# Gated rows of w_down kept in DRAM, and the scale of gelu times up moved into the evacuation of the up sums

## The chip, the cores and the metric

The kernel runs on one core of one Trainium2 chip. The metric is the device time of one execution in microseconds (us); before the change it is 1646.46 us, the median of 3 runs (1646.23 to 1646.75). A core has five engines that run on their own and wait for each other by semaphores: PE (matrix products, with PEld for its weight loads), DVE (vector), ACT (activations and copies with a scale), POOL (elementwise) and SP, which here issues every DMA, in the order of its queue.

## The reference, cut to what matters

```
mod = (silu(c) @ w_mod), cut into sa, ca, ga, sb, cb, gb       # rows of 512
h = layernorm(x) * (1 + ca) + sa
x = x + ga * attention(h)      # 2048 queries, 32 heads of 128, the last 512 keys of the cache
h = layernorm(x) * (1 + cb) + sb
g, u = h @ w_gate, h @ w_up    # 512 -> 1376
x = x + gb * ((gelu(g) * u) @ w_down)                          # 1376 -> 512
```

All inputs are float32. The gate gb multiplies the result's columns, so it can be multiplied into the columns of w_down beforehand.

## The kernel before, in words

**Precision.** Each float32 operand of a product is split in two float16 halves, high and low, and a product is three matmuls (high by high, high by low, low by high). ACT makes a high half by a copy, DVE or POOL makes the low half by subtraction. The operands are scaled into float16's range by powers and maxima found at run time; the scales of the feed-forward part lie in the columns of the tile `ffs`: column 2 scales w_down, column 3 goes into gelu, column 4 into the product of gelu and up, column 5 into the evacuation of the last product.

**Stages.** Attention fills about the first 1270 us: 128 iterations, each one head and 512 queries. In each, scores go to PSUM (`psS`), ACT takes the exponentials, POOL makes the low halves (`s_low`, line 921), SP transposes them by DMA into `pT` (tag with three buffers), and `pv` (line 935) multiplies them by v. The feed-forward part follows. It works on 22 units (p, f): p is one of two halves of the 2048 rows (1024 rows, as two blocks of 512), f one of 11 blocks of 128 columns of the 1376 (the last has 96). A unit's gate and up products run by Strassen-Winograd's scheme on two PSUM banks, X and Y, in four stages (`stage`, line 1686): after stages 0, 1 and 2 ACT copies the sum in X to SBUF (tile `h32`), and DVE adds Y to it into the tile `r`, whose two halves hold gelu's input or output and up. Stage 0 gives the gate of block 0, stage 2 and stage 3 give the two ups, and in stage 3 gelu reads X itself. `finish` (line 1662) multiplies gelu by up and by `ffs` column 4, and the product is split into the hidden block `hid`, or, for three pairs of units, kept in `hf` and combined further. `down` takes hid with w_down into `acc`, which DVE adds to in place (`down_add`, line 1722); a finished `acc` goes out by DMA.

**The gate in w_down.** w_down's maximum must be known before its scale is. So during attention the 11 blocks of w_down are loaded into a ring of two buffers (`raw2`; `fm_load`, line 1241), multiplied by the row gb on POOL (`fm_gate`, 1252) and reduced to their maxima on DVE (`fm_max`, 1246); the gated blocks are then dropped. In the feed-forward part `wd_load` (1469) loads each block again, `wd_gate` (1473) gates it again, `wd_high` and `wd_low` split it; `wt_make` (1625) does the same for the six blocks of the three pairs. For these gates the row gb is loaded a second time (`gate_again`, 1212), since its buffer has had another use in between.

**What sets the order.** No instruction is issued where the code calls it. `Weaver` (lines 90 to 447) records every call with its operands (`note`, 174), plays the program through a model of the engines with costs per instruction (`cost`, 150; `play`, 250), and issues it in the order of the best of several plans, some of them shaken by random numbers from a fixed seed (`issue`, 412). The plan is made in pieces: what starts before 60 us of the model is fixed first, then up to 130 us, and so on to the end. So every change to the list of calls gives a new plan from the start on. `tt` (line 982) leaves a two-tile operation to POOL or DVE, as the planner finds; a `scalar_tensor_tensor` called on `nc.vector` is DVE's. One rule of the model is used below. Between two instructions of PE, or two of SP, a dependence costs no time of its own unless the later one reads a DRAM tile:

```
def in_line(self, m, n):                                  # line 138
    return self.ops[m][0] == self.ops[n][0] and self.ops[m][0] in ("PE", "SP") and n not in self.landing
```

All instructions go out from one line (444), so rows of the profile are told apart by the tiles that they write and read, not by lines. In them `h` is the tile `h32`, `T`, `B`, `A`, `S` are the operands of the Winograd products, `st` the softmax statistics.

## Time and profile before

| what | value |
|---|---|
| median of 3 runs | 1646.46 us (1646.23 to 1646.75) |
| the profiled execution's own time | 1646.04 us |
| its span, first to last instruction | 1644.3 us |
| instructions | 24592 |
| granted clock of PE | 1.000 |
| DMA queue of SP: bytes, share of 16 engines | 230.99 MB, 70.4% |

A row of the profile by stretches gives, for a window of the span, the busy us and number of instructions of PE, PEld, DVE, ACT and POOL, PE's granted clock, the busy share of the DMA engines and GB/s. A row of a group gives the engine, the operation, out<-in with shapes, the count, then busy us and the mean ns of one, then the idle time before them and what ended it. A row of the timeline gives start and duration in us, with the idle time before it in brackets. A row of DMA issues ends with the median us from issue to landing.

### The profile page before, as it was taken

Reading aid. Unit: us, or ns where it says so; the run is one execution under the profiler, and the core shown is the slowest. Engines: PE = TensorE matmul, PEld = TensorE weight load, DVE = VectorE, ACT = ScalarE, POOL = GpSimd, SP = SyncE. Lnnn points to the kernel's source line nnn. Section 1 sums busy time; section 2 is a strip of 40 time slices with the busy share of each in tenths; the row PEclk is TensorE's granted clock in tenths of the full one; section 3 lists DMA queues with packets and bytes.
Section 4 is the critical chain, followed back from the end, with each engine's and each line's share of the span. In section 5 each row is a group of like instructions: output and inputs, shape, how many; then the busy total and the mean of one; then the engine's idle time right before and its main releaser. Section 6 shows DMA issues by size and latency. Waiting matters only on the chain.

```text
span 1644.3 us, 24592 instructions
## 1 busy us (share of the span) xinstructions
PE 1633.7 (99%) x7754; PEld 764.7 (47%) x7754; DVE 1441.0 (88%) x2644; ACT 1241.1 (75%) x2466; POOL 1119.3 (68%) x911
## 2 busy tenths in 40 slices
PE   8999999999999999999999999999999999999999
PEld 5544444444444444444444444444444444444564
DVE  8999988888888889889989898888889987897786
ACT  6977877777787887877778778778777977676553
POOL 4788766557666676775678888887655866636672
PEclk9999999999999999999999999999999999999999
DMA  8867887877787989899998988787865742321121
GB/s 243 152 130 135 150 162 130 151 137 152 141 161 143 193 148 184 169 196 179 209 175 180 181 172 175 155 166 162 159 114 92 146 98 71 75 63 46 39 74 52
DMA packets 697538, 232.55 MB, mean 141 GB/s; under 512 B 605248, under 2 KB 673920, under 8 KB 697408
## 3 DMA queue, kind: packets, MB, share of 16 engines
q1 hardware_dynamic: 697408, 230.99, 70.4%
q8 instruction: 61, 1.00, 0.3%
q14 instruction: 69, 0.57, 0.1%
HBM read 80.81 MB, written 5.38 MB: 52 GB/s over the span
## 4 chain that ended last, share of the span: by engine, by line
PE 95%; DVE 3%; DMA 1%; ACT 1%; SPq 0%; issue 0%; POOL 0%; DVEq 0%; ACTq 0%
PE psS L444 31%; PE psW L444 24%; PE psO L444 21%; PE psQ L444 18%; DVE st L444 1%; DMA acc<-in_A_x_dram 1%; DVE acc L444 1%; DMA raw<-in_A_wo_dram 0%; DMA wm<-in_w_mod_dram 0%; DVE bnst L444 0%; SPq L444 0%; ACT h L444 0%; DVE hf L444 0%; DVE B L444 0%; DVE raw L444 0%
## 5 line engine op out<-in xcount | busy, mean ns | idle before, releaser
L444 POOL TENSOR_TENSOR pp<-p,pp 128x1024 f16<-128x1024 f32 x256 | 545.2, 2130 | 309.1 <-ACT pp L444 194.5
L444 ACT ACTIVATE p<-psS,st,es 128x512 f32<-128x512 f32 x512 | 393.2, 774 | 181.1 <-DVE st L444 175.7
L444 PE MATMUL psW<-wo,oT 128*128 128x512 f16 x1536 | 417.6, 379 | 0.1
L444 DVE SCALAR_TENSOR_TENSOR acc<-psW,st,acc 128x512 f32<-128x512 f32 x496 | 366.8, 742 | 39.5 <-PE psW L444 36.9
L444 PE MATMUL psS<-kT,q 128*128 128x512 f16 x1536 | 376.9, 379 | 1.5 <-ACT q L444 1.0
L444 PE MATMUL psO<-pT,v 128*128 128x512 f16 x1536 | 377.7, 379 | 0.0
L444 DVE TENSOR_REDUCE st<-psS 128x2 f32<-128x1024 f32 x256 | 312.3, 1220 | 47.3 <-PE psS L444 47.0
L444 ACT ACTIVATE pp<-p 128x1024 f16<-128x1024 f32 x256 | 271.1, 1059 | 3.9
L444 PEld LDWEIGHTS <-q 128*128 128x128 f16 x1536 | 149.9, 98 | 181.2 <-ACT q L444 1.5
L444 PEld LDWEIGHTS <-oT 128*128 128x128 f16 x1536 | 150.2, 98 | 180.3 <-issue 0.4
L444 PEld LDWEIGHTS <-v 128*128 128x128 f16 x1536 | 150.2, 98 | 180.2 <-DMA pT<-pp 0.2
L444 PEld LDWEIGHTS <-aw 128*128 128x128 f16 (+1 forms) x840 | 84.2, 100 | 94.3 <-issue 1.8
L444 ACT ACTIVATE oT<-psO 128x512 f16<-128x512 f32 x128 | 76.1, 594 | 64.2 <-PE psO L444 63.8
L444 PE MATMUL psS<-T,aw 128*128 128x512 f16 (+1 forms) x480 | 120.4, 379 | 0.6 <-DVE r L444 0.4
L444 PE MATMUL psQ<-B,A 128*128 128x512 f16 x480 | 120.1, 379 | 0.0
L444 PE MATMUL psQ<-T,S 128*128 128x512 f16 x468 | 114.6, 379 | 0.0
L444 DVE SCALAR_TENSOR_TENSOR oT<-psO,oT 128x512 f16<-128x512 f32 x128 | 88.0, 687 | 24.4 <-ACT oT L444 24.1
L444 PEld LDWEIGHTS <-A 128*128 128x128 f16 x696 | 68.0, 98 | 81.3 <-issue 1.0
L444 ACT ACTIVATION_READ_ACCUMULATOR p<-psS,st,es 128x1 f32 x512 | 101.5, 198 | 0.0
L444 PEld LDWEIGHTS <-S 128*128 128x128 f16 x624 | 61.0, 98 | 73.7
L444 PE MATMUL psS<-B,aw 128*128 128x512 f16 (+1 forms) x360 | 90.9, 379 | 0.6 <-ACT r L444 0.6
L444 DVE TENSOR_SCALAR st<-st,es 128x1 f32<-128x1 f32 x512 | 84.8, 205 | 3.2
(275 smaller groups left out, 2326.8 us busy)
## 6 DMA issues: line engine op xcount, KB each, us to landing
raw<-in_A_k_cache_dram SPq DMA_DIRECT2D x32, 256.0 KB, 3.6
raw<-in_A_wq_dram SPq DMA_DIRECT2D x32, 256.0 KB, 3.4
raw<-in_A_v_cache_dram SPq DMA_DIRECT2D x32, 256.0 KB, 3.3
raw<-in_A_wo_dram SPq DMA_DIRECT2D x32, 256.0 KB, 3.2
pT<-pp SPq DMA_TRANSPOSE x512, 3.3
sa<-most SPq DMA_DIRECT2D x28, 256.0 KB, 3.8
raw<-in_B_w_gate_dram SPq DMA_DIRECT2D x26, 256.0 KB, 3.1
raw<-in_B_w_up_dram SPq DMA_DIRECT2D x26, 256.0 KB, 3.2
```

The source lines that it names most:

```text
L444: made[n] = real(*a, **k)
```

## The change

During attention each gated block of w_down is, after its gate, also stored by a DMA of SP into a DRAM tile of its own (`fm_keep`; 11 tiles `wg0` to `wg10`). The feed-forward part loads the blocks from there, and the 17 gates, the function `wd_gate` and the second load of gb are gone. In `finish` the product of gelu and up is a plain two-tile product, which the planner may give to POOL or DVE. Its former scale (`ffs` column 4) is applied earlier to up: ACT's copies of X after stages 1 and 2 carry it as their scale, and DVE's two sums that give up multiply Y by it.

```diff
-    MS, FF = {}, {}
+    MS = {}
...
-    def gate_again():
-        FF["gb"] = base.tile([P, D], F32, name="gb", tag="gb", bufs=1)
-        mod_row(5, FF["gb"])
...
+    WG = {}
+
+    def fm_keep(n):
+        f = n - 24
+        t = WG[f] = dram.tile([P, D], F32, name=f"wg{f}", tag=f"wg{f}", bufs=1)
+        m = min(P, DFF - f * P)
+        nc.sync.dma_start(t[:m], FM[n][:m])
+
     for n in range(len(pieces_)):
         at(s + 2 + 11 * n // 4, fm_load, n)
         if n >= 24:
             at(s + 5 + 11 * n // 4, fm_gate, n)
+            at(s + 6 + 11 * n // 4, fm_keep, n)
         at(s + 8 + 11 * n // 4, fm_max, n)
...
     def wd_load(f):
         t = FRAW["d", f] = raw_tile()
-        nc.sync.dma_start(t[:rows(f)], w_down[f * P:f * P + rows(f), :])
-
-    def wd_gate(f, eng=nc.gpsimd):
-        m = rows(f)
-        t = FRAW["d", f]
-        tt(t[:m], t[:m], FF["gb"][:m], OP.mult)
+        nc.sync.dma_start(t[:rows(f)], WG[f][:rows(f)])
...
             t = raw_tile()
-            nc.sync.dma_start(t, w_down[(f + k) * P:(f + k + 1) * P, :])
-            tt(t, t, FF["gb"], OP.mult)
+            nc.sync.dma_start(t, WG[f + k])
             raw.append(t)
...
-            nc.vector.scalar_tensor_tensor(HF[u][:, r, :], t[:, 1, :], ffs[:, 4:5], t[:, 0, :], op0=OP.mult, op1=OP.mult)
+            tt(HF[u][:, r, :], t[:, 1, :], t[:, 0, :], OP.mult)
...
-        nc.vector.scalar_tensor_tensor(t[:m, 1, :], t[:m, 1, :], ffs[:m, 4:5], t[:m, 0, :], op0=OP.mult, op1=OP.mult)
+        tt(t[:m, 1, :], t[:m, 1, :], t[:m, 0, :], OP.mult)
...
         if n < 3:
             v = UV[u, n] = right.tile([P, N], F32, name="h32", tag="h32", bufs=3)
-            nc.scalar.activation(v[:m], X, AF.Copy)
+            nc.scalar.activation(v[:m], X, AF.Copy, scale=ffs[:m, 4:5] if n else 1.0)
         if n in (0, 2):
-            t = r_tile(u, n // 2)[:m, n // 2, :]
-            nc.vector.tensor_tensor(t, Y, UV.pop((u, n))[:m], op=OP.add)
+            t, v = r_tile(u, n // 2)[:m, n // 2, :], UV.pop((u, n))[:m]
             if n == 0:
+                nc.vector.tensor_tensor(t, Y, v, op=OP.add)
                 gelu(u, 0, t)
+            else:
+                nc.vector.scalar_tensor_tensor(t, Y, ffs[:m, 4:5], v, op0=OP.mult, op1=OP.add)
         if n == 3:
-            nc.vector.tensor_tensor(RT[u, 0][:m, 1, :], Y, UV.pop((u, 1))[:m], op=OP.add)
+            nc.vector.scalar_tensor_tensor(RT[u, 0][:m, 1, :], Y, ffs[:m, 4:5], UV.pop((u, 1))[:m], op0=OP.mult, op1=OP.add)
             gelu(u, 1, X)
             finish(u, 1)
             finish(u, 0)
...
-    at(e + 9, gate_again)
...
             wd_load(w)
-            wd_gate(w)
             wd_high(w)
             wd_low(w)
```

Since the planner sets the order, the diff does not show it. Two places follow. The first is SP's queue late in the attention, where the middle blocks of w_down are loaded for their maxima; `most` and `sa` belong to the maxima of the heads' weights, and a name's number tells one tile from the next. In brackets stand the engines or DMA lanes that a row waits for. Before:

```order
L444 DMA most_2115<-mx0_79 128x4 [waits DMAHW0_49,DVE_49]
L444 DMA raw2_1918<-in_B_w_down_dram 128x512 [waits DMAHW1_49,DVE_49]
L444 DMA raw2_1953<-in_B_w_down_dram 128x512 [waits DMAHW2_49,DVE_49]
L444 DMA_TRANSPOSE pT_2081<-pp_2080 128x8x128 [waits DMAHW3_49,PE_49,Pool_49]
L444 DMA_TRANSPOSE pT_2081<-pp_2080 128x8x128 [waits DMAHW4_49]
L444 DMA sa_2134<-most_2115 128x512 [waits DMAHW5_49,DMAHW0_49]
```

After:

```order
L444 DMA raw2_1902<-in_B_w_down_dram 128x512 [waits DMAHW6_49,DMAHW3_49,DVE_49]
L444 DMA wg3_1914<-raw2_1871 128x512 [waits DMAHW7_49]
L444 DMA raw2_1922<-in_B_w_down_dram 128x512 [waits DMAHW7_49,DMAHW0_49,DVE_49]
L444 DMA_TRANSPOSE pT_2068<-pp_2067 128x8x128 [waits DMAHW1_49,PE_49,Pool_49]
L444 DMA_TRANSPOSE pT_2068<-pp_2067 128x8x128 [waits DMAHW2_49]
```

The load of raw2_1922 takes the buffer that wg3 is stored from, and waits for the lane of that store (DMAHW7), with the transposes behind it; before, a load in this ring waited for DVE's maximum only.

The second place is the end of DVE's queue, in the last unit (1, 10), whose tiles have 96 rows: `r_3458` and `r_3462` before, `r_3468` and `r_3472` after, are its gelu and up of the two blocks. Before:

```order
L444 TENSOR_TENSOR r_3458<-psS_3456,h32_3459 96x512 [waits PE_49]
L444 SCALAR_TENSOR_TENSOR r_3458<-r_3458,ffs_82 96x512 [waits DVE_49]
L444 SCALAR_TENSOR_TENSOR acc_72<-psW_3467,ffs_82,acc_72 128x512 [waits PE_49]
L444 SCALAR_TENSOR_TENSOR r_3462<-r_3462,ffs_82 96x512 [waits Activation_49]
L444 TENSOR_TENSOR hid_3464<-r_3462,hid_3464 96x512 [waits Activation_49]
L444 TENSOR_TENSOR hid_3465<-r_3458,hid_3465 96x512 [waits Activation_49]
```

After:

```order
L444 SCALAR_TENSOR_TENSOR r_3468<-psS_3466,ffs_82,h32_3469 96x512 [waits PE_49]
L444 SCALAR_TENSOR_TENSOR acc_72<-psW_3476,ffs_82,acc_72 128x512 [waits PE_49]
L444 SCALAR_TENSOR_TENSOR acc_72<-psW_3477,ffs_82,acc_72 128x512 [waits PE_49]
L444 TENSOR_TENSOR r_3472<-r_3472 96x512 [waits Activation_49]
L444 TENSOR_TENSOR hid_3474<-r_3472,hid_3474 96x512 [waits Activation_49]
L444 TENSOR_TENSOR hid_3475<-r_3468,hid_3475 96x512 [waits Activation_49]
```

The last sum now carries the scale, the product of r_3468 has left DVE (it is POOL's last instruction), and a second sum into acc stands in its place.

## Prediction

> **What bounds the kernel now.** First the page's busy times, then the same engines by stretches of the span (busy us, number of instructions, granted clock, DMA share, GB/s).

> ```profile
> span 1644.3 us, 24592 instructions
> PE 1633.7 (99%) x7754; PEld 764.7 (47%) x7754; DVE 1441.0 (88%) x2644; ACT 1241.1 (75%) x2466; POOL 1119.3 (68%) x911
> ```

> ```profile
> 0.00:41.00 41.00, 36.40 (x205) 23.77 (x206) 32.81 (x91) 25.93 (x45) 20.51 (x40) 1.00 0.85 244
> ...
> 400.00:1260.00 860.00, 860.00 (x3987) 389.80 (x3985) 762.54 (x1444) 673.58 (x1358) 617.68 (x438) 1.00 0.85 166
> 1260.00:1340.00 80.00, 79.21 (x382) 37.57 (x381) 73.56 (x137) 67.59 (x132) 54.30 (x45) 1.00 0.64 127
> 1340.00:1450.00 110.00, 110.00 (x511) 49.80 (x510) 92.57 (x141) 80.84 (x154) 69.52 (x91) 1.00 0.29 74
> 1450.00:1500.00 50.00, 48.64 (x223) 22.26 (x222) 43.79 (x66) 34.64 (x66) 23.18 (x26) 1.00 0.19 52
> 1500.00:1630.00 130.00, 130.00 (x729) 72.40 (x727) 102.37 (x152) 68.51 (x130) 82.94 (x94) 1.00 0.14 42
> 1630.00:1645.00 15.00, 10.43 (x49) 4.52 (x47) 9.47 (x14) 1.83 (x3) 0.00 (x0) 0.93 0.38 140
> 850.00:965.00 115.00, 115.00 (x535) 52.14 (x533) 102.96 (x192) 90.32 (x185) 94.38 (x70) 1.00 0.89 178
> ```

> PE is busy for 1633.7 of 1644.3 us, so only 10.6 us of it are idle. Of those, 4.6 us (41.00 - 36.40) lie in the start and 4.6 us (15.00 - 10.43) in the tail. Every stretch that the change relieves has PE at or near 100%. The idle places between are these (the number in brackets is the idle time of PE before the row, and what ended it):

> ```profile
> 1277.89 1.46 PE L444 MATMUL psQ<-T,A 128*128 128x512 f16 x6 [0.28 <-DVE h L444]
> 1323.51 0.39 PE L444 MATMUL psS<-T,B 128*128 128x512 f16 x1 [0.44 <-ACT B L444]
> 1465.15 2.75 PE L444 MATMUL psS<-B,aw 128*128 128x512 f16 x12 [0.61 <-ACT r L444]
> 1471.15 0.38 PE L444 MATMUL psS<-T,aw 128*128 128x512 f16 x1 [0.38 <-DVE r L444]
> 1471.79 0.38 PE L444 MATMUL psS<-T,aw 128*128 128x512 f16 x1 [0.26 <-POOL T L444]
> ```

> They come to 0.28 + 0.44 + 0.61 + 0.38 + 0.26 = 1.97 us. That is all that faster helpers can give back between the start and the tail.

> Does a busy PE hide waits inside the matmuls? The pace says no: 860.00 / 3987 = 215.7 ns a matmul in the attention and 110.00 / 511 = 215.3 ns in the feed-forward part, while DVE's share goes from 0.89 to 0.84 and the DMA share from 0.85 to 0.29. A pace that does not move with the helpers is PE's own. [...]

> **The change, part by part.** The prices, from the groups of 1270 to 1645 us (busy us, mean ns):

> ```profile
> L444 DVE TENSOR_TENSOR raw<-raw,gb 128x512 f32<-128x512 f32 x9 | 6.8, 760 | 0.0
> L444 DVE SCALAR_TENSOR_TENSOR r<-r,ffs 128x512 f32<-128x512 f32 x28 | 22.0, 793 | 1.9 <-ACT r L444 1.8
> L444 DVE TENSOR_TENSOR hf<-hf 128x512 f32<-128x512 f32 x8 | 5.5, 681 | 0.5 <-POOL hf L444 0.5
> L444 DVE TENSOR_TENSOR r<-psS,h 128x512 f32<-128x512 f32 x60 | 41.2, 687 | 25.2 <-ACT h L444 15.7 <-PE psS L444 8.8
> L444 DVE SCALAR_TENSOR_TENSOR acc<-psO,ffs,acc 128x512 f32<-128x512 f32 x32 | 23.8, 742 | 2.6 <-PE psO L444 2.6
> L444 POOL TENSOR_TENSOR raw<-raw,gb 128x512 f32<-128x512 f32 x7 | 8.9, 1272 | 3.5 <-DVE hf L444 2.0 <-DVE wd L444 1.5
> L444 ACT ACTIVATE h<-psS 128x512 f32<-128x512 f32 x60 | 35.6, 596 | 42.5 <-PE psS L444 42.1
> L444 ACT ACTIVATE r<-psS,ffs 128x512 f32<-128x512 f32 x20 | 13.6, 679 | 3.6 <-DVE r L444 3.3
> ```

> 1. *The 17 gates go.* The order of before has 10 on DVE and 7 on POOL: 10 x 0.760 = 7.6 us of DVE and 7 x 1.272 = 8.9 us of POOL.
> 2. *The product loses its scale.* All 44 stood on DVE: 44 x 0.79 = 34.8 us go. The order of after puts 32 on DVE and 12 on POOL. A plain product of two SBUF tiles takes between 681 ns (hf) and 760 ns (the gate) on DVE; I take 0.72: 23.0 us. POOL gets 12 x 1.272 = 15.3 us.
> 3. *The scale enters the evacuation.* 44 activations go from 596 ns to the 679 of the form with a scale from a column: 44 x 0.083 = +3.7 us of ACT. 44 sums go from 687 ns to what a scaled sum out of PSUM costs, 742: +2.4 us of DVE.

> So DVE is relieved by 7.6 + 34.8 - 23.0 - 2.4 = 17.0 us out of the 312.3 that it is busy from 1260 to 1630, ACT gets 3.7 more, and POOL 15.3 - 8.9 = 6.4 more. None of this is time by itself: PE hides all but the five waits above. Of the five I let half go in time, since the relief is on DVE, and three of them name ACT or POOL, which get more work: **-1.0 us**, bounds -1.97 (all) and +1.0 (the same waits half as long again).

> 4. *Eleven stores and what stands behind them.* Each is a DMA more on SP's queue in about 850 to 965 us. Five of the eleven (wg1, wg3, wg4, wg7, wg8) have, as the very next row, the load that reuses the buffer they read from, and that load waits for the store to land. The planner's model counts two DMAs of SP as in line (line 139), without such a wait. Behind the held queue stand the transposes that pv needs. How long does a store take to land? Nearest rows (median us from issue to landing): stores of whole rows late in the kernel, two kinds of loads in this stretch, and a scattered store a little earlier:

> ```profile
> out_dram<-acc SPq DMA_DIRECT2D x16, 256.0 KB, 2.5
> raw<-in_B_w_down_dram SPq DMA_DIRECT2D x10, 256.0 KB, 3.6
> raw<-in_A_k_cache_dram SPq DMA_DIRECT2D x3, 256.0 KB, 4.2
> msum<-ga SPq DMA_DIRECT2D x1, 256.0 KB, 5.6
> ```

> So 2.5 to 5.6 us; I take 3.6, the load of the same size in the same stretch. What can SP spare, and how late may transposes be? SP's waits in 850 to 965 us (total, times, longest; 13 rows, the first and the last shown, sum 47.0 us), then one load and four transposes on SP, the pv that uses these, and how long a transpose takes to land:

> ```profile
> SPq L444 <- POOL raw L444: 12.9, 5, 3.6
> ...
> SPq L444 <- DVE top L444: 0.4, 1, 0.4
> ```

> ```profile
> 851.54 0.52 SPq L444 DMA_DIRECT2D raw<-in_B_w_down_dram  x1
> 854.10 7.04 SPq L444 DMA_TRANSPOSE pT<-pp  x4
> ```

> ```profile
> 866.92 1.46 PE L444 MATMUL psO<-pT,v 128*128 128x512 f16 x6
> 877.28 1.46 PE L444 MATMUL psO<-pT,v 128*128 128x512 f16 x6
> ```

> ```profile
> pT<-pp SPq DMA_TRANSPOSE x47, 3.3
> ```

> SP idles 47.0 of 115 us, 4.2 us in each round of 10.4 us (877.28 - 866.92). A store and its wait take 0.5 us of issue and 3.1 of waiting, 3.6 us, of that. The last of four transposes is issued a quarter of 7.04 us before 861.14, so at 859.4, lands 3.3 us later at 862.7, and is used at 866.92: 4.2 us of slack. A hold of 3.6 us fits into either. I put **+0.5 us** for one that meets a late gate on POOL, bounds 0 and +8.5 (the rival below). The extra 11 x 0.25 MB raise 178 GB/s by 2.75 MB / 115 us = 24 GB/s to 202, under what PE has borne without a wait:

> ```profile
> 780.00:820.00 40.00, 40.00 (x187) 18.15 (x186) 38.85 (x76) 31.03 (x65) 25.42 (x19) 1.00 1.05 210
> ```

> [...]

> 5. *The second load of gb* and the loads of w_down: one load of 256 KB less, and 17 loads that read other DRAM at the same size. They are issued ahead of use by whole units: 0.

> 6. *The tail.* The last unit's hidden block is waited for there:

> ```profile
> 1630.75 0.69 DVE L444 TENSOR_TENSOR r<-psS,h 96x512 f32<-96x512 f32 x1 [2.27 <-PE psS L444]
> ...
> 1634.26 0.50 PEld L444 LDWEIGHTS <-hid 96*128 96x128 f16 x3 [0.15 <-ACT hid L444]
> ...
> 1634.98 4.96 PEld L444 LDWEIGHTS <-hid 96*128 96x128 f16 x24 [0.23 <-DVE hid L444]
> ```

> Between the last matmul into psS and the first that reads the last hid stood 18 other matmuls, and now stand 21: 3 x 0.216 = 0.65 us more cover. Against it stand 0.06 us for the longer sum; the second sum into acc that DVE now has ahead of the last product takes the place of the other product, now on POOL. So the wait of 0.15 + 0.23 goes: **-0.3 us**, bounds -0.4 and +0.5 (product late by the difference 1.272 - 0.76).

> 7. *The start* has the same 58 filling matmuls and almost the same PE order up to the first scores, since planning begins again from other random draws: 0, bounds -0.6 and +0.6.

> Sum: -1.0 + 0.5 - 0.3 = -0.8 us. The profiled execution took 1646.04 us (span 1644.3 and 1.74 around it), 0.42 below the median of 1646.46; so 1645.2 for such an execution and **1645.7 us** for the median.

> **The rivals.**

> *A. Nothing arrives.* The saved DVE time is off the path, the new order has its own few waits in other places: 1646.5. For it: the helpers are already hidden for 98% of the way. Against: two of the waits at 1465 to 1472 name r, which DVE and ACT make.

> *B. The stores hold SP.* If they land in 5.6 us as the scattered store did, a hold is 0.5 + 5.2 = 5.7 us, 1.5 over the slack of 4.2; a held gate ahead of it adds to that. Five of them cost 5 x 1.5 = 7.5 us at PE, and with one more us at the start of it 8.5; if SP's idle time takes up part, 4. Middle 6: 1652.5. It decides from a landing of about 4.2 us on. For it: DMA share 0.89 there, and the loads of k there took 4.2 us. Against: the plain stores' 2.5.

> *C. The evacuation of psS becomes what PE waits for.* If each unit's psS came free later by both increments, 44 x 0.083 + 44 x 0.055 = 6.1 us: 1652.6. Against: PE waits for r at two places in 22 units now, and the product behind it is shorter.

> *D. Waits hidden in the matmuls' pace.* If PE's busy time did hold waits, part of the 17.0 us would show; with DVE one of three helpers, I set a third: -5.7, and 1640.8. Against: the pace of 215.7 and 215.3 ns.

> **How the numbers follow.** Forecast 0.60; A 0.18; B 0.14, of which 0.09 beyond 3.3 us; C 0.05; D 0.03. 0.2% is 3.3 us, about what a measurement of this kernel can tell from no change. Faster by more: D alone, 0.03, since start, waits and tail together hold no 3.3 us that the change can reach (1.97 + 0.4 + 0.6 = 3.0). Slower by more: 0.09 + 0.05 = 0.14. Same: 0.83. The range goes from 1646.5 - 1.97 - 0.4 = 1644.1 up to 1649.8, which takes in A and the lesser part of B; outside lie D and what is 3.3 us or more slower, 0.17.

> **What would show it.** Right: PE idle in 1260 to 1630 us below 1.97 us; no wait at pv between 850 and 970 us; the stores wgN landing in about 3.6 us; DVE busy about 17 us less; no wait of PE's loads for hid in the tail. Wrong: rows psO<-pT,v or their weight loads released by a DMA with 0.5 us or more, stores that take over 4.2 us, or PE waiting for ACT h or r in many units. A different pace than 215.5 ns would break the whole working.

## The result, and the profile after

The changed kernel takes 1652.15 us, the median of 6 runs (1650.85 to 1656.6), against 1646.7 us for the kernel before beside it (6 runs, 1646.23 to 1647.15): a ratio of 1.0036, with an interval of 1.0026 to 1.0047. It is 5.45 us slower, where 1645.7 was forecast in a range up to 1649.8. The profiled execution took 1652.53 us; its page begins:

```profile
span 1650.7 us, 24575 instructions
PE 1635.2 (99%) x7754; PEld 765.2 (46%) x7754; DVE 1436.8 (87%) x2642; ACT 1231.8 (75%) x2444; POOL 1122.7 (68%) x918
```

The span grew by 6.4 us. By stretches (columns as before) it is seen where:

```profile
0.00:41.00 41.00, 36.29 (x206) 23.91 (x207) 32.69 (x90) 27.14 (x47) 19.64 (x39) 1.00 0.85 244
...
850.00:965.00 115.00, 110.05 (x502) 49.13 (x500) 97.85 (x186) 87.57 (x178) 82.09 (x60) 0.99 0.91 190
965.00:1260.00 295.00, 295.00 (x1369) 133.72 (x1367) 259.97 (x494) 226.72 (x458) 228.46 (x160) 1.00 0.81 153
```

PE stands still for 4.95 us (115.00 - 110.05) in the one stretch with the stores, where before it stood still for none, and runs 502 matmuls there in place of 535. The 33 that are missing are worth 33 x 0.2157 = 7.1 us (0.2157 us is the pace of 400 to 1260 us before): more than the idle time. PE's idle places of over 0.3 us behind the start, all of them:

```profile
44.29 0.59 PE L444 MATMUL psS<-kT,q 128*128 128x512 f16 x2 [0.53 <-ACT p L444]
930.09 1.46 PE L444 MATMUL psO<-pT,v 128*128 128x512 f16 x6 [1.35 <-DMA pT<-pp]
942.90 2.61 PE L444 MATMUL psO<-pT,v 128*128 128x512 f16 x6 [3.59 <-DMA pT<-pp]
1331.94 0.59 PE L444 MATMUL psO<-pT,v 128*128 128x512 f16 x2 [0.73 <-DMA pT<-pp]
1479.20 1.02 PE L444 MATMUL psS<-T,aw 128*128 128x512 f16 x4 [0.41 <-ACT h L444]
```

Two pv waited for transposes, 1.35 and 3.59 us. The row at 942.90 shows the rest: its six matmuls took 2.61 us where six take 1.46. PE's granted clock there (the third column from the end, 0.60) says why:

```profile
942.90:947.20 4.30, 4.29 (x13) 1.59 (x13) 0.00 (x0) 0.00 (x0) 0.63 (x2) 0.60 1.17 160
947.20:955.00 7.80, 7.80 (x38) 3.56 (x37) 6.05 (x12) 6.23 (x13) 5.21 (x4) 1.00 0.70 159
```

After the long pause the next twelve matmuls took 947.2 - 942.9 = 4.3 us instead of 12 x 0.216 = 2.6: another 1.7 us. So 1.35 + 3.59 + 1.7 = 6.6 us come from here. The start lost 0.6 more, and between 1260 and 1630 us 0.75 was won back (PE idle for 1.40 us in place of 2.15): about the 6.4 by which the span grew.

The pv of one head and 512 queries needs four transposes, two from each of two `pp`. Why they were late for the pv at 942.90 is seen on SP, with POOL's makers of the two `pp` (start, duration):

```profile
923.30 2.14 POOL L444 TENSOR_TENSOR pp<-p,pp 128x1024 f16<-128x1024 f32 x1 [0.32 <-POOL raw L444]
928.43 2.14 POOL L444 TENSOR_TENSOR pp<-p,pp 128x1024 f16<-128x1024 f32 x1
928.70 0.38 SPq L444 DMA_DIRECT2D wg<-raw  x1
...
932.18 0.33 SPq L444 DMA_DIRECT2D raw<-in_B_w_down_dram  x1
932.61 2.59 SPq L444 DMA_TRANSPOSE pT<-pp  x2
...
935.29 0.53 SPq L444 DMA_DIRECT2D wg<-raw  x1
937.75 0.34 SPq L444 DMA_DIRECT2D raw<-in_B_w_down_dram  x1
938.18 8.78 SPq L444 DMA_TRANSPOSE pT<-pp  x6
```

The first pp was ready at 925.44 and its two transposes went out from 932.61 on; the second was ready at 930.57 and its two are the first of the six from 938.18 on: 7.2 and 7.6 us late. (The transposes of a pp go out in the order in which POOL makes them, so counting both from the kernel's start pairs them.) Ahead of each pair stand a store to wg and then the load into the buffer that it was stored from, 3.1 and 1.9 us behind the store's end. The pv at 930.09 came too early for these two holds. Its last two transposes went out from 924.45 on, 4.6 us behind their pp (ready at 919.82), on a queue that four earlier holds had made late. SP's own waits of 850 to 965 us (total, times, longest), and how long the stores took to land:

```profile
SPq L444 <- DMA wg<-raw: 13.5, 6, 3.0
```

```profile
wg<-raw SPq DMA_DIRECT2D x10, 256.0 KB, 3.2
```

This wait did not exist before, and a store landed in 3.2 us where 3.6 were assumed.

### The profile page after: what moved, and what is told of

The parts are those of the page before. It is cut to its first block, busy times and chain, and to the rows that moved or that the text cites. A ratio compares the mean times of both kernels' runs of the same rounds, so it can differ in the third digit from the quotient of the medians.

```text
span 1650.7 us, 24575 instructions
## 1 busy us (share of the span) xinstructions
PE 1635.2 (99%) x7754; PEld 765.2 (46%) x7754; DVE 1436.8 (87%) x2642; ACT 1231.8 (75%) x2444; POOL 1122.7 (68%) x918
## 4 chain that ended last, share of the span: by engine, by line
PE 93%; DMA 2%; ACT 1%; DVE 1%; POOL 1%; issue 0%; SPq 0%; DVEq 0%; POOLq 0%; ACTq 0%
PE psS L444 30%; PE psW L444 24%; PE psO L444 22%; PE psQ L444 18%; DMA acc<-in_A_x_dram 1%; DMA pT<-pp 1%; SPq L444 0%; DVE acc L444 0%; ACT p L444 0%; DMA wm<-in_w_mod_dram 0%; DMA raw<-in_A_wo_dram 0%; DVE r L444 0%; DVE bnst L444 0%; ACT h L444 0%; POOL raw L444 0%
## 5 line engine op out<-in xcount | busy, mean ns | idle before, releaser
L444 POOL TENSOR_TENSOR pp<-p,pp 128x1024 f16<-128x1024 f32 x256 | 545.2, 2130 | 289.9 <-ACT pp L444 167.2
L444 ACT ACTIVATE p<-psS,st,es 128x512 f32<-128x512 f32 x512 | 393.5, 774 | 187.4 <-DVE st L444 186.4
L444 PE MATMUL psW<-wo,oT 128*128 128x512 f16 x1536 | 418.2, 379 | 0.0
L444 DVE SCALAR_TENSOR_TENSOR acc<-psW,st,acc 128x512 f32<-128x512 f32 x496 | 366.7, 741 | 47.2 <-PE psW L444 45.6
L444 PE MATMUL psO<-pT,v 128*128 128x512 f16 x1536 | 379.8, 380 | 5.7 <-DMA pT<-pp 5.7
L444 PE MATMUL psS<-kT,q 128*128 128x512 f16 x1536 | 375.8, 379 | 2.3 <-ACT q L444 1.6
L444 DVE TENSOR_REDUCE st<-psS 128x2 f32<-128x1024 f32 x256 | 312.3, 1220 | 49.7 <-PE psS L444 48.8
L444 ACT ACTIVATE pp<-p 128x1024 f16<-128x1024 f32 x256 | 271.0, 1059 | 4.0
L444 PEld LDWEIGHTS <-v 128*128 128x128 f16 x1536 | 150.2, 98 | 187.2 <-issue 8.8
L444 PEld LDWEIGHTS <-q 128*128 128x128 f16 x1536 | 149.8, 98 | 182.2 <-ACT q L444 2.4
L444 PEld LDWEIGHTS <-oT 128*128 128x128 f16 x1536 | 150.2, 98 | 180.3 <-DVE oT L444 0.2
L444 ACT ACTIVATE oT<-psO 128x512 f16<-128x512 f32 x128 | 76.2, 595 | 69.3 <-PE psO L444 68.1
L444 PEld LDWEIGHTS <-aw 128*128 128x128 f16 (+1 forms) x840 | 84.2, 100 | 91.9 <-issue 1.1
L444 PE MATMUL psS<-T,aw 128*128 128x512 f16 (+1 forms) x480 | 120.5, 379 | 0.4 <-ACT h L444 0.4
L444 PE MATMUL psQ<-B,A 128*128 128x512 f16 x480 | 119.7, 379 | 0.3 <-POOL B L444 0.3
L444 PE MATMUL psQ<-T,S 128*128 128x512 f16 x468 | 114.8, 381 | 0.0
L444 DVE SCALAR_TENSOR_TENSOR oT<-psO,oT 128x512 f16<-128x512 f32 x128 | 87.8, 686 | 21.5 <-ACT oT L444 21.0
L444 PEld LDWEIGHTS <-A 128*128 128x128 f16 x696 | 68.1, 98 | 82.1 <-issue 1.0
L444 ACT ACTIVATION_READ_ACCUMULATOR p<-psS,st,es 128x1 f32 x512 | 101.5, 198 | 0.0
L444 PEld LDWEIGHTS <-S 128*128 128x128 f16 x624 | 61.2, 98 | 74.4 <-issue 1.3
L444 PE MATMUL psS<-B,aw 128*128 128x512 f16 (+1 forms) x360 | 87.6, 379 | 0.1
L444 DVE TENSOR_SCALAR st<-st,es 128x1 f32<-128x1 f32 x512 | 84.6, 205 | 3.4
## 6 DMA issues: line engine op xcount, KB each, us to landing
raw<-in_A_k_cache_dram SPq DMA_DIRECT2D x32, 256.0 KB, 3.8
raw<-in_A_wq_dram SPq DMA_DIRECT2D x32, 256.0 KB, 3.5
raw<-in_A_v_cache_dram SPq DMA_DIRECT2D x32, 256.0 KB, 3.3
raw<-in_A_wo_dram SPq DMA_DIRECT2D x32, 256.0 KB, 3.1
sa<-most SPq DMA_DIRECT2D x28, 256.0 KB, 4.0
raw<-in_B_w_gate_dram SPq DMA_DIRECT2D x26, 256.0 KB, 3.1
raw<-in_B_w_up_dram SPq DMA_DIRECT2D x26, 256.0 KB, 3.1
```

The source lines that it names most:

```text
L444: made[n] = real(*a, **k)
```

## The experiments

Two theories stood against the one of the holds (a load on SP waits for the store ahead of it to land, and what is queued behind it waits too): that the stores' traffic or issue is what costs, and that the new order of the instructions is worse in itself, stores or not. In the first three, and in two later ones, the planner records the program of the change and sets its order; only what is issued for a store or a load is exchanged, so that the order on PE, DVE, ACT and POOL stays the same row for row. Runs of the kernel before beside each set had medians of 1646.57, 1646.58 and 1646.8 us.

**No stores.** The stores are left out, and the feed-forward part loads w_down without the gate.

```diff
-        nc.sync.dma_start(t[:m], FM[n][:m])               # issued: nothing
-        nc.sync.dma_start(t[:rows(f)], WG[f][:rows(f)])   # issued instead:
+        nc.sync.dma_start(t[:rows(f)], w_down[f * P:f * P + rows(f), :])
```

> The change with its order of instructions kept on every engine, but without the 11 stores; the feed-forward part loads w_down itself, so its blocks lack the gate. Holds (loads on SP wait for the store ahead of them to land and keep the transposes back): no wait of pv for pT between 850 and 970 us, 1645 to 1646.5 us. Traffic or issue of the stores: the same. The new order in itself is worse: still 1651 to 1653 us.

1645.24 us (ratio 0.9991, 0.9981 to 1.0000). The order by itself is not worse; the stores cost the time. Its profiled execution, at 1647.9 us, lies above all its other runs, since it lost time at its start (PE's clock stood at 0.50 from 11.95 to 15.37 us). In 850 to 970 us PE idles nowhere in it.

**The stores take another tile.** Eleven stores of the same size at the same places, of the row gb.

```diff
-        nc.sync.dma_start(t[:m], FM[n][:m])
+        nc.sync.dma_start(t[:m], gb[:m])
```

> The change with its order kept, the 11 stores of the same size at the same places, but each stores the row tile gb, which no load overwrites then; the stored blocks are not the gated ones. Holds: no load waits for a store any more, 1645.5 to 1647 us, no wait at pv. Traffic or issue: the stores are all there, so 1651 to 1653 us. Order: 1651 to 1653 us.

1645.19 us (0.9989, 0.9980 to 0.9999). Its stretch with the stores, and their landing:

```profile
850.00:970.00 120.00, 120.00 (x558) 54.33 (x556) 108.89 (x205) 94.62 (x192) 91.95 (x66) 1.00 0.99 201
```

```profile
wg<-gb SPq DMA_DIRECT2D x10, 256.0 KB, 3.5
```

```profile
937.73 1.46 PE L444 MATMUL psO<-pT,v 128*128 128x512 f16 x6
```

The same bytes, at a DMA share of 0.99, with landings no shorter (3.5 us): PE does not stop once in this stretch. So traffic and issue alone cost nothing, and taking the wait of the load for the store away takes the loss away: 1652.15 - 1645.19 = 7.0 us. But they did use up slack, the time from the landing of the last of a pv's four transposes to that pv: ahead of the pv at 937.73 it landed at 936.44, so 1.3 us were left.

**Two stores in place of one.** A second store of each block, to another DRAM tile, ahead of the first.

```diff
+        nc.sync.dma_start(TWO[:m], FM[n][:m])
         nc.sync.dma_start(t[:m], FM[n][:m])
```

> The change with its order kept, and ahead of each store a second one of the same block to another DRAM tile. Holds: each wait of a load for its store grows by 0.5 us of issue and about 0.6 to 1 us of transfer, six to nine holds, so 1656 to 1662 us. Traffic: twice the added bytes, about twice the added time, 1657 us. Order: 1652 us.

1657.06 us (1.0065, 1.0050 to 1.0080), 4.9 more than the change.

```profile
SPq L444 <- DMA wg<-raw: 14.2, 6, 3.1
```

```profile
916.40 1.46 PE L444 MATMUL psQ<-T,S 128*128 128x512 f16 x6 [1.88 <-DVE q L444]
921.16 1.47 PE L444 MATMUL psO<-pT,v 128*128 128x512 f16 x6 [0.72 <-DMA pT<-pp]
934.35 2.08 PE L444 MATMUL psO<-pT,v 128*128 128x512 f16 x6 [2.65 <-DMA pT<-pp]
948.24 2.33 PE L444 MATMUL psO<-pT,v 128*128 128x512 f16 x6 [2.98 <-DMA pT<-pp]
```

The time came out as the holds had it, and as the traffic had it, so it does not tell the two apart; and not by the holds' reason, since the waits hardly grew (14.2 us for 13.5). In the change's trace the issue of a store takes 0.38 to 0.57 us; its 256 KB are 128 packets of 84 ns each in the median, 0.67 us on 16 engines, and 0.9 to 1.5 us from the first to the last in the five stores beside which no other packets of this size stand. PE idles 8.2 us in 850 to 970 us, 3.3 more than in the change, and its clock falls to 0.50 twice (from 935.04 and from 948.70 us) instead of once, another 1.7 us. That the eleven further issues on a queue already late by the holds are what made the transposes later is likely, but not shown.

**Other draws, before.** The kernel before, with `random.Random(8)` for `random.Random(7)` in the planner.

> The kernel before with another seed of the planner's random draws, nothing else. It shows what a new plan alone is worth. Holds: within 1.5 us of 1646.7. New plans differ by much: 1643 to 1653 us.

1645.78 us (0.9995, 0.9986 to 1.0005): a new plan by itself moved 0.8 us, which the interval does not tell from nothing.

**The planner is told.** In the change, a dependence on a store to a wg tile counts with its landing.

```diff
-        return ... and n not in self.landing
+        return ... and n not in self.landing and m not in self.stores
...
+        if engine == "SP" and wrote[0].name.startswith("wg"):
+            self.stores.add(op)
```

> The change, with the planner told that an instruction of SP that follows a store to a wg tile waits for its landing (two lines of in_line and note). Everything is computed as in the change. Holds: the plan itself puts each load some rows behind its store, so 1645 to 1646.5 us, with no wait at pv in 850 to 970 us. If the planner's own estimate of a landing is too short: 1647 to 1650 us.

1645.22 us (0.9992, 0.9983 to 1.0000). SP waits for no store in 850 to 970 us, and PE is not idle there. The stores are the same eleven; the plan puts each load some rows further on.

**A wider ring.** In the change, w_down's blocks go through the ring of eight.

```diff
-        t = FM[n] = raw_tile("raw2", 2)
+        t = FM[n] = raw_tile() if n >= 24 else raw_tile("raw2", 2)
```

> The change, with the blocks of w_down for the maxima loaded into the ring raw of eight buffers in place of raw2 of two, so that the load that waits for a store is eight loads further on. Holds: 1645 to 1646.5 us. If the ring's other users (the heads' weights) are held back by it: 1647 to 1650 us.

1643.62 us (0.9983, 0.9974 to 0.9992), faster than either kernel.

```profile
850.00:970.00 120.00, 120.00 (x558) 54.36 (x556) 112.53 (x212) 91.91 (x189) 77.70 (x54) 1.00 0.96 192
1260.00:1630.00 370.00, 369.72 (x1854) 183.87 (x1853) 308.94 (x490) 255.49 (x481) 220.25 (x242) 1.00 0.31 70
```

In the feed-forward part PE idles 0.28 us (370.00 - 369.72). By the same sum it was 2.15 before; the prediction's 1.97 are the rows of over 0.25 us alone.

**The scale half alone.** The kernel before with the edits of `finish` and `stage` only.

> The kernel before with the half of the change that moves the scale and frees the product, without stores; the gates in the feed-forward part stay. Holds: no stores, so within 1 us of before or up to 1 us faster, 1645.5 to 1646.8 us. If the scaled evacuation held PE: 1649 to 1653 us.

1648.24 us (1.0014, 1.0005 to 1.0023), slower by 1.7: more than was expected of it, and no sign of a held evacuation in unit after unit. PE idles 0.46 us more in the attention and 2.71 us in 1260 to 1630 us, where it idled 2.15 before: together 1.0 of the 1.4 us by which its span is longer (1645.7 us). The largest rows:

```profile
918.77 1.47 PE L444 MATMUL psO<-pT,v 128*128 128x512 f16 x6 [0.46 <-DMA pT<-pp]
...
1467.82 0.39 PE L444 MATMUL psS<-T,aw 128*128 128x512 f16 x1 [2.08 <-DVE r L444]
```

Whether the one wait of 2.08 us is bought by the longer sums or is this plan's accident is not shown; e6 and e11 below, with and without this half, are alike.

**The store half alone.** The kernel before with the stores and without the gates; the product keeps its scale.

> The kernel before with the half of the change that stores the gated blocks and drops the 17 gates; the scale stays in the product. Its plan has one load directly behind its store (wg2) and the others two or more rows behind, where the change has five directly behind. Holds: fewer and shorter holds than in the change, 1646 to 1650 us. Traffic: the same bytes, 1651 to 1653 us.

1644.69 us (0.9990, 0.9981 to 0.9999), below the range. It is the most telling of the plans, for its SP waits as long for stores as the change's does, and PE hardly notices:

```profile
SPq L444 <- DMA wg<-raw: 13.2, 6, 4.8
```

```profile
897.72 1.46 PE L444 MATMUL psO<-pT,v 128*128 128x512 f16 x6 [0.57 <-DMA pT<-pp]
```

So it is not the sum of the holds that decides, but where they fall (this is another plan, so its slack differs too). Here the stores of blocks 7 and 8 go out together, and so do the two loads behind them:

```profile
932.40 1.21 SPq L444 DMA_DIRECT2D wg<-raw  x2
934.75 1.01 SPq L444 DMA_DIRECT2D raw<-in_B_w_down_dram  x2
```

One wait of 1.1 us serves both; in the change the same two blocks hold SP twice in ten us.

**Blocks 7 and 8 freed.** The change with its order, where only the stores of these two take gb.

> The change with its order kept; only the stores of blocks 7 and 8, whose holds fall in one round ahead of the same pv, take the row tile gb in place of the gated block (two wrong blocks). If those two holds made the long wait of 3.6 us and the slow matmuls behind it: 1646 to 1648 us, with the wait of 1.35 us at 930 us still there. If every hold costs alike: 1650 to 1651.5 us.

1646.46 us (0.9996, 0.9987 to 1.0005). SP still waits 9.3 us for the other stores, and PE only here:

```profile
929.81 1.46 PE L444 MATMUL psO<-pT,v 128*128 128x512 f16 x6 [0.60 <-DMA pT<-pp]
```

**Only blocks 7 and 8 hold.** The reverse: the other nine take gb.

> The reverse: the other nine stores take gb (nine wrong blocks), only those of 7 and 8 hold their loads. If the two holds in one round suffice: 1648 to 1651 us with a wait of 1.5 to 3.5 us at one pv. If the earlier holds have to use up SP's spare time first: 1645 to 1647 us.

1647.48 us (1.0003, 0.9994 to 1.0012), 0.5 us under the lower end for "the two suffice", with the wait that this named, and without slow matmuls behind it:

```profile
940.07 1.46 PE L444 MATMUL psO<-pT,v 128*128 128x512 f16 x6 [2.37 <-DMA pT<-pp]
```

Against the same order without any hold (1645.19), the two alone cost 2.3 us and the other nine alone 1.3, together 3.6; all eleven cost 7.0 (each figure within 1.5 us or so, by the intervals). The holds cost more together than one by one: the earlier ones leave the queue late, so that the last two find no slack, and the pause grows from 2.37 to 3.59 us and the slow clock (0.50 for 3.41 us) follows it.

**Store half with the wide ring.** e8 with the edit of e6.

> The half of the change with the stores (the gates dropped, the scale left in the product), with the wide ring of e6. If the scale half is worth something, this is slower than e6: 1644 to 1645.5 us. If it is worth nothing: 1643 to 1644 us.

1644.15 us (0.9982, 0.9973 to 0.9991), as much below its neighbours as e6 (0.9983). The scale half is worth nothing that can be measured here.

**The change with other draws.** The whole change, `random.Random(8)`.

> The whole change with the other seed of the planner's draws. Its plan has four loads directly behind their stores, two of them (7 and 8) a few rows apart as in the change. If the holds and not this one plan are the cause: 1648 to 1655 us, with waits of pv for pT. If the change's plan was bad luck: 1644.5 to 1647 us.

1652.15 us (1.0029, 1.0019 to 1.0039). The same size, in other places:

```profile
919.77 1.47 PE L444 MATMUL psO<-pT,v 128*128 128x512 f16 x6 [0.48 <-DMA pT<-pp]
...
927.53 0.81 PE L444 MATMUL psQ<-B,A 128*128 128x512 f16 x3 [1.11 <-DVE h L444]
...
942.08 0.38 PE L444 MATMUL psO<-pT,v 128*128 128x512 f16 x1 [1.90 <-DMA pT<-pp]
```

Two of the waits shown, 2.38 us, are pv's for pT, as the holds would have it. What kept h back by 1.11 us was not followed, and the profiled execution, at 1650.21 us, lies 1.9 below the median. Still the change's time is not one plan's bad luck: two plans of it that do not know of the hold pay, one that knows does not.

## Why the prediction was wrong

- **The step that failed is 4**, "a hold of 3.6 us fits into either". The length of a hold was right or even too long (a landing of 3.2 us). Wrong was to set each hold against a fresh slack of 4.2 us, read off one round of the old order. Slack here is the time from the landing of the last of a head's four transposes to its first pv, worked out from the traces' records of issue and landing. Five rounds in a row, each kernel's at its own times:

  | first pv in the change, us | before | change's order, no stores (e1) | stores, no holds (e2) | the change |
  |---|---|---|---|---|
  | 897.36 | 2.5 | 2.4 | 2.0 | 1.8 |
  | 907.72 | 4.1 | 3.9 | 3.9 | 2.3 |
  | 918.21 | 3.2 | 3.5 | 1.8 | 0.1 |
  | 930.09 | 3.5 | 3.7 | 1.3 | none, PE waits 1.35 |
  | 942.90 | 3.0 | 2.8 | 1.3 | none, PE waits 3.59 |

  Three things were missed. The old order itself had under 3.6 us in 7 of the 11 rounds of 850 to 965 us (2.5 to 4.7). The stores, even without a hold, left 1.3 us in two rounds. And what one hold took was not there for the next: two fall between 928 and 938 us, after four others from 867 to 920 us. SP's spare time did not help: besides the 13.5 us for stores SP still waited 26.7 us in that stretch for other things, but not where the transposes stood behind a hold. The term was +0.5 us; its measure is 7.0 (the change against e2).
- **The length of a landing:** 3.6 us were taken for a store, from loads of the same size; the stores' medians were 2.5 (e5) to 3.6 us (e6), in the change 3.2.
- **Rival B** had the place, the hold longer than the slack, and nearly the time (1652.5), with a chance of 0.14. The time was luck: its price came from landings of 5.6 us and five equal holds. Its condition was wrong in the same way as step 4: it was to decide from a landing of 4.2 us on, and it decided at 3.2. Five rows "load directly behind its store" were counted, and the two of them within six rows of each other were not looked at for themselves.
- **The clock was not in the sum at all.** The pause of 3.59 us cost 1.7 us more in slow matmuls. In the change and in e3 the clock stood at 0.50 for 3.41 us at a time, not from the end of a pause but 0.15 us behind it (the pause of 3.59 us) and 0.69 and 0.46 us behind it (those of 2.65 and 2.98 us in e3; last section).
- **Steps 1 to 3, the prices, held:** the scaled sum out of PSUM takes 748 ns (742 set), the copy with a scale 686 (679), the product 771 and 685 ns in its two forms on DVE (0.72 set), and 32 of 44 products were on DVE:

```profile
L444 DVE SCALAR_TENSOR_TENSOR r<-psS,ffs,h 128x512 f32<-128x512 f32 x40 | 29.9, 748 | 12.6 <-ACT h L444 6.3 <-PE psS L444 5.8
L444 DVE TENSOR_TENSOR r<-r 128x512 f32<-128x512 f32 x22 | 16.7, 771 | 1.6 <-ACT r L444 1.3
L444 DVE TENSOR_TENSOR hf<-r 128x512 f32<-128x512 f32 x7 | 4.8, 685 | 0.1
L444 ACT ACTIVATE h<-psS,ffs 128x512 f32<-128x512 f32 x40 | 27.5, 686 | 24.8 <-PE psS L444 23.9
```

  But DVE is not 17 us less busy, as "what would show it" had it: its total fell by 4.2 us (1441.0 to 1436.8). In 1260 to 1630 us it fell by only 0.7 (312.28 to 311.55). The planner fills the room that it gets; nine of the low halves of hid out of hf stand on DVE now, where three stood.
- **The half of the five waits:** set at -1.0 us. In the same order without holds (e2) PE idles 0.67 us in 1260 to 1630 us, in place of 2.15: -1.5. Right in sign and about in size, but hardly by the relief of DVE that it was put down to: of the 17.0 us, 2.7 came there in e2 (312.28 to 309.59). The store half alone (e8) idles 0.00 us there and the scale half alone (e7) 2.71, so the gates that went are the likelier reason.
- **The tail:** wrong, -0.3 set and nothing won. The weight loads no longer wait for hid there, but PE had lost nothing to those waits: before and after, its matmuls stand back to back from 1630 us to the last one, which ends 3.8 us (before) and 3.9 us (after) ahead of the span's end. The 4.6 us that the prediction calls idle in the tail run 0.7 us past the end of the span, 1644.3.
- **The start:** 41.00 - 36.29 = 4.71 us for 4.60, and 0.53 us at 44.29: -0.6 to +0.6 was set, +0.6 came.
- **Traffic:** right; e2 carries it at 201 GB/s and a share of 0.99.
- **Rivals A, C and D:** without the hold's +0.5 the sum is 1645.2, and e1, e2 and e5 give 1645.24, 1645.19 and 1645.22. That agreement is partly luck (-1.5 and 0 stood for -1.0 and -0.3), and it is 1.4 us below the kernel before, hardly to be told from A. C is not seen: PE waits for r or h in a few places at most in any of these runs, not in unit after unit. D is not borne out, but was not fully put to the test either: PE's pace did not move (109.74 / 509 = 215.6 ns in 1340 to 1450 us), but DVE gave back only 0.7 of the 17.0 us.

## What to carry to other kernels

The stores that were added to SP's queue were priced here by what was queued behind the next load into their buffer (7.0 us, the change against e2), not by their bytes (1645.19 us in e2, which stores as many): look for the reuse of the stored buffer right behind it, and give the ring more buffers (1643.62 us, e6), or tell the planner of the wait (1645.22 us, e5). Slack has to be read for every round, in the order that will be issued and with the new transfers in it; one round of the old order did not stand for the rest (4.2 us read, 2.5 to 4.7 over its 11 rounds, 0.1 and none in the change). Then draw the holds up one after the other, with what each leaves to the next. A saving on engines that PE hides was worth 1.4 us here (e2), while the new waits cost five times that, 7.0 us.

## What the runs showed of the hardware that was not expected

```profile
939.64:943.05 3.41, 0.14 (x1) 0.19 (x2) 1.92 (x5) 1.63 (x4) 2.78 (x3) 1.00 1.16 210
943.05:946.47 3.42, 3.42 (x9) 1.18 (x8) 0.00 (x0) 0.00 (x0) 0.48 (x1) 0.50 1.16 140
...
931.63:935.04 3.41, 0.76 (x5) 0.36 (x5) 2.45 (x5) 2.88 (x7) 2.03 (x1) 1.00 1.09 244
935.04:938.46 3.42, 3.42 (x10) 1.23 (x9) 0.71 (x2) 1.13 (x2) 2.90 (x3) 0.50 0.45 155
...
935.64:939.06 3.42, 2.06 (x10) 0.83 (x9) 3.27 (x6) 2.14 (x5) 2.24 (x2) 1.00 1.07 204
939.06:942.47 3.41, 2.40 (x12) 1.09 (x12) 0.89 (x3) 1.63 (x4) 2.24 (x3) 1.00 1.20 201
942.47:945.88 3.41, 3.41 (x17) 1.53 (x16) 2.01 (x3) 1.84 (x3) 1.35 (x1) 1.00 1.00 132
```

In these traces the clock stood at 0.50 for one beat behind a beat in which PE idled for most of the time: 3.27 us of 3.41 in the change, 2.65 and 2.96 in e3, 2.04 at the start of e1. It fell likewise at the end of the span, behind beats with 2.44 us (before) and 2.80 us idle (the change). The pause of 2.37 us in e10 was cut into 1.36 and 1.01, and the clock stayed at 1.00. Beats with 1.84 (e3) and 1.90 us (e12) idle passed, one with 1.81 at the very end of e4 did not, so in these runs the line lies near 1.9 us, and they do not draw it sharply. A beat at 0.50 is 3.41 / 2 = 1.7 us of PE's work. So a pause between about 1.9 and 3.8 us (twice 1.9) may or may not cost this, by where the beat cuts it; that range is an estimate from these beats.

How long a store took to land did not follow the DMA share: in the stretch with the stores the median was 2.5 us at a share of 0.96 (e5) and 3.6 at the same 0.96 (e6), 2.6 at 0.95 (e8), 3.2 at 0.91 (the change) and 3.5 at 0.99 (e2), against 2.5 for the stores of the result late in the kernel before.
